# Handing out GpSimd's weight sums one at a time, and moving two small sums in VectorE's queue, in a fused RWKV-5 and SwiGLU kernel

## The chip, the cores and the metric

One core of a Trainium2 chip. The time is device microseconds (us) of one execution. The engines are called TensorE (PE in the profile; PEld is its weight load), VectorE (DVE), ScalarE (ACT) and GpSimd (POOL). A stop is idle time of TensorE in front of an instruction. The granted clock is the share of its full speed that TensorE was given in a stretch; 0.50 is called half clock here. PSUM is the memory that TensorE writes its results to, which VectorE and ScalarE then empty. Work is on the path when the end of the run comes later by as much as the work does.

## The reference

Attention of the RWKV-5 kind over 4 batches of 768 positions with 8 heads of 48, then a gated feed-forward block (384 to 1536 to 384) on the 3072 tokens that come out. All data are float32.

```python
def _attn_ref(r, k, v, w, u):
    B, H, S, D = r.shape                      # 4, 8, 768, 48
    state = np.zeros((B, H, D, D), dtype=np.float32)
    for t in range(S):
        kt, vt, rt = (k[:, :, t], v[:, :, t], r[:, :, t])
        cur = np.einsum('bhd,bhe->bhde', u[None] * kt, vt)
        y[:, :, t] = np.einsum('bhd,bhde->bhe', rt, state + cur)
        state = w[None, :, :, None] * state + np.einsum('bhd,bhe->bhde', kt, vt)

def _moe_ref(x, w_gate, w_val, w_out):
    g = x @ w_gate
    silu = g * (1.0 / (1.0 + np.exp(-g)))
    return (silu * (x @ w_val) @ w_out).astype(np.float32)
```

## The kernel before

Attention is computed in 24 chunks of 128 positions. For each chunk a matrix At of 128x128 per head holds the scores; its diagonal is `du`, the sum over a head's 48 columns of r·k·u. GpSimd forms the product `rk`, VectorE sums it to `du`, and ScalarE writes `ident` times `du` into At. The scores then overwrite one side of At, and the matmuls into `y_ps` use it.

```python
    def own_product(i):
        kl, rl = k_ld[i % 2], r_ld[i % 2]
        rk = two.tile([P, H, D], FP32, name="rk", tag="rk")       # two buffers
        pool.tensor_mul(rk[:], rl[:], kl[:])
        pool.tensor_mul(rk[:], rk[:], ub[:])
        du = three.tile([P, H], FP32, name="du", tag="du")
        dve.tensor_reduce(du[:], rk[:], axis=AX.X, op=ALU.add)
        dus[i] = du

    def diagonal(i):
        du = dus.pop(i)
        ...                                                        # i < 2: on GpSimd
            for h in range(H):
                act.activation(At[i % 2][:, h, :], ident[:], AF.Identity, scale=du[:, h : h + 1])
```

Beside this the weights are rounded in chunks by three engines. ScalarE writes `w_mag` (one buffer) and `w_low`, VectorE a `tensor_scalar` and a `scalar_tensor_tensor` per half, GpSimd the closing addition:

```python
        dve.tensor_scalar(dst, hi, -(1 << 31), None, ALU.bitwise_and)
        dve.scalar_tensor_tensor(
            dst, mags[n][half], 3, dst, ALU.logical_shift_left, ALU.bitwise_or)
        ...
            pool.tensor_tensor(dst, dst, low, ALU.add)
```

Gate units (`gate_value`: six matmuls with `wg`, six with `wv` into `gv`, a sigmoid `sg` on ScalarE, two products `sg` and `hT` on VectorE) fill TensorE's time between. The last projection is done with seven products of halves instead of eight; it needs four sums of weight halves and four of `hT` per pair of chunks, all on GpSimd:

```python
    def weight_sums():
        pool.tensor_sub(wt[1][:], w22, w12)
        pool.tensor_sub(w12, w12, w11)
        pool.tensor_sub(wt[0][:], w22, w12)
        pool.tensor_sub(wt[2][:], w21, wt[0][:])
```

The loop over steps, cut; "F" in `gaps` feeds a unit, "R" rounds a chunk of weights:

```python
    EARLY = {s: ("R", "F", "R", "F", "RF") for s in range(3, 12)}
    ...
    for s in range(3, N + 2):
        if s <= N:
            diagonal(s - 1)
        if s + 1 < N:
            own_product(s + 1)
            scale(s + 1)
        if s < N:
            turn(s)                    # transposes tp, then kT and rT on ScalarE
        gaps(s, 0)
        if s <= N:
            scores(s - 1, 0)
            ...
        gaps(s, 2)
        if s >= 4:
            outputs(s - 2)             # y_ps
            ...
        gaps(s, 4)
        if s == 12:
            count_outside()            # three on VectorE, n_ps on TensorE
        if done["pool"] == NW and not summed:
            weight_sums()
```

## Time and profile before

| what | before |
|---|---|
| time, median of 3 runs | 707.17 us (706.67 to 707.88) |
| span of the profiled execution | 706.3 us |
| TensorE busy, 0 to 195 us | 175.39 of 195.00 us |
| TensorE busy, 195 to 690 us | 495.00 of 495.00 us |
| TensorE busy, 690 us to the end | 10.56 of 16.30 us |

The three stretches are from the table of windows. All slack of TensorE lies in the first and the last; the middle can only get worse. The list of waits and the timelines of the first stretch are shown in the prediction.

### The profile page before, as it was taken

To read this page: it belongs to the slowest core of one execution; us is meant where nothing else is said; L and a number is where in the kernel's file an instruction comes from. 1 tells how busy PE (TensorE), PEld (TensorE's weight loads), DVE (VectorE), ACT (ScalarE), POOL (GpSimd) and SP (SyncE) were. 2 spreads that over 40 slices of the span, in tenths; PEclk is the share of its full clock that TensorE was granted. 3 is DMA by queue.
4 is the path that set the end of the run, shared out by engine and by line. 5 is a ranking of instruction groups with operands and counts; after the bars stand their busy time and mean duration, and the time that the engine had idled before them with its cause. 6 is when DMAs were issued, how large, how long until landed. Compare 5 with 4: busy or idle time off the path is not lost.

```text
span 706.3 us, 11610 instructions
## 1 busy us (share of the span) xinstructions
PE 681.0 (96%) x4822; PEld 620.2 (88%) x4822; DVE 240.7 (34%) x519; ACT 204.4 (29%) x522; POOL 237.1 (34%) x191
## 2 busy tenths in 40 slices
PE   8888997999899999999999999999999999999996
PEld 8777886898798998999999999999898998998996
DVE  5777772313222222323222322323222322222222
ACT  3577762442132231313131331313131211111110
POOL 6877678358203320602512420602400400304000
PEclk9998998999999999999999999999999999999999
DMA  8798831113001010102011110001000000000000
GB/s 236 196 240 226 204 76 34 35 35 78 17 18 46 12 34 23 34 1 57 12 23 35 23 35 23 12 1 35 1 1 23 1 1 23 1 17 7 1 23 26
DMA packets 85774, 34.07 MB, mean 48 GB/s; under 512 B 76368, under 2 KB 79568, under 8 KB 85712
## 3 DMA queue, kind: packets, MB, share of 16 engines
q1 hardware_dynamic: 82256, 28.52, 17.3%
q10 hardware_dynamic: 3456, 4.72, 1.8%
q8 instruction: 40, 0.66, 0.4%
q14 instruction: 22, 0.18, 0.1%
HBM read 28.51 MB, written 4.72 MB: 47 GB/s over the span
## 4 chain that ended last, share of the span: by engine, by line
PE 81%; DVE 6%; POOL 5%; ACT 5%; issue 1%; DMA 1%; SPq 0%; DVEq 0%; POOLq 0%
PE gv L390 47%; PE o_a L453 13%; PE o_b L453 10%; PE y_ps L344 4%; PE s_ps L314 4%; PE tp L300 2%; ACT At L291 2%; ACT w_mag L162 1%; PE u_ps L357 1%; DVE At L318 1%; ACT kT L303 1%; DVE hT L398 1%; DVE sg L397 1%; DVE wg L180 1%; DMA r_ld<-in_r_dram 1%
## 5 line engine op out<-in xcount | busy, mean ns | idle before, releaser
L390 PE MATMUL gv<-xT,wg 128*128 128x256 f32 x864 | 216.0, 387 | 4.0 <-DVE hT L398 4.0
L390 PE MATMUL gv<-xT,wv 128*128 128x256 f32 x864 | 211.6, 381 | 0.0
L390 PEld LDWEIGHTS gv<-xT,wv 128*128 128x128 f32 x864 | 165.5, 192 | 22.9
L390 PEld LDWEIGHTS gv<-xT,wg 128*128 128x128 f32 x864 | 159.7, 193 | 25.8 <-issue 7.7
L397 DVE TENSOR_TENSOR sg<-sg,gv 128x256 f32<-128x256 f32 x144 | 60.5, 420 | 348.2 <-ACT sg L396 347.8
L396 ACT ACTIVATE sg<-gv 128x256 f32<-128x256 f32 x144 | 55.0, 382 | 345.9 <-PE gv L390 345.8
L432 POOL TENSOR_TENSOR hs<-hT 128x768 f32<-128x768 f32 x11 | 19.9, 1809 | 195.6 <-DVE hT L398 195.6
L370 POOL TENSOR_TENSOR Z<-Z,wL 96x384 f32<-96x384 f32 x16 | 15.9, 995 | 191.7 <-DVE Z L369 191.7
L398 DVE TENSOR_TENSOR hT<-sg,gv 128x256 f32<-128x256 f32 x144 | 60.6, 421 | 5.1
L291 ACT ACTIVATE At<-ident,du 128x128 f32<-128x128 f32 x176 | 53.6, 389 | 0.0
L314 PE MATMUL s_ps<-rT,kT 96*128 96x128 f32 x384 | 51.3, 278 | 0.4 <-DVE Z L367 0.4
L453 PE MATMUL o_a<-wt,hs 128*128 128x192 f32 x288 | 50.9, 327 | 0.4 <-ACT u L461 0.4
L314 PEld LDWEIGHTS s_ps<-rT,kT 96*128 96x128 f32 x384 | 49.5, 194 | 1.5 <-DVE Z L367 0.7
L453 PE MATMUL o_b<-wo,hs 128*128 128x192 f32 x288 | 50.7, 326 | 0.0
L453 PEld LDWEIGHTS o_a<-wt,hs 128*128 128x128 f32 x288 | 47.5, 190 | 1.5 <-ACT u L461 0.7
L453 PEld LDWEIGHTS o_b<-wo,hs 128*128 128x128 f32 x288 | 47.6, 190 | 0.8
L318 DVE COPY_PREDICATED At<-mask,s_ps 128x512 f32<-128x512 int32 x48 | 35.0, 733 | 24.4 <-PE s_ps L314 24.4
L344 PE MATMUL y_ps<-At,v_ld 128*32 128x128 f32 x768 | 36.1, 279 | 5.8 <-ACT kT L303 4.4
L344 PEld LDWEIGHTS y_ps<-At,v_ld 128*32 128x32 f32 x768 | 29.9, 111 | 6.6 <-ACT kT L303 4.6
L344 PE MATMUL y_ps<-rT,Z 96*32 96x128 f32 x480 | 30.2, 278 | 1.7 <-ACT kT L303 1.7
L303 ACT ACTIVATE kT<-tp,own 96x512 f32<-96x512 f32 x48 | 29.8, 672 | 0.0
L162 ACT ACTIVATE w_mag<-w_bits 128x384 f32<-128x384 f32 x36 | 19.0, 529 | 24.3 <-DVE wg L180 11.0
(82 smaller groups left out, 639.2 us busy)
## 6 DMA issues: line engine op xcount, KB each, us to landing
k_ld<-in_k_dram SPq DMA_DIRECT2D x24, 192.0 KB, 2.9
r_ld<-in_r_dram SPq DMA_DIRECT2D x24, 192.0 KB, 3.3
w_bits<-in_moe_w_gate_dram SPq DMA_DIRECT2D x6, 768.0 KB, 5.1
v_ld<-in_v_dram SPq DMA_DIRECT2D x48, 96.0 KB, 2.8
w_bits<-in_moe_w_val_dram SPq DMA_DIRECT2D x6, 768.0 KB, 4.7
w_bits<-in_moe_w_out_dram SPq DMA_DIRECT2D x6, 768.0 KB, 4.5
out_dram<-o_sb ACTq DMA_DIRECT2D x24, 192.0 KB, 1.9
ub<-in_u_dram SPq DMA_DIRECT2D x1, 192.0 KB, 3.7
```

The costliest lines, as they stand in the source:

```text
L162: act.activation(mags[n][-1].bitcast(FP32), hi.bitcast(FP32), AF.Abs, scale=float(2.0**-112))
L291: act.activation(At[i % 2][:, h, :], ident[:], AF.Identity, scale=du[:, h : h + 1])
L303: act.activation(kT[i % 2][:, :, e, :], tp[0:D2], AF.Identity, scale=own[:, e : e + 1])
L314: pe.matmul(ps[:, n, :], kT[i % 2][:, a, e, :], turned[i][:, a, :], start=True, stop=True, skip_group_check=True,)
L318: dve.copy_predicated(At[i % 2][:, 4 * half : 4 * half + 4], mask[:].bitcast(INT32).unsqueeze(1).to_broadcast([P, HP, P]), ps[:],)
L344: pe.matmul(ps[32 * q : 32 * q + 32, cc, :], *rows[q][n], start=(n == 0), stop=(n == len(rows[q]) - 1), skip_group_check=True,)
L390: pe.matmul(gv[:, o, :].rearrange("p (i t) -> p i t", i=2), wt[:, c, P * f : P * (f + 1)], xT[:, 2 * g % NX : 2 * g % NX + 2, c, :], start ...
L396: act.activation(sg[:], gv[:, 0, :], AF.Sigmoid)
L397: dve.tensor_mul(sg[:], sg[:], gv[:, 0, :])
L398: dve.tensor_mul(hT[g][:, f, :], sg[:], gv[:, 1, :])
L432: by.tensor_add(s1, h22, h21)
L453: pe.matmul(ps[:], lhs[:, f, :], rhs[:, f, :], start=(f == 0 and n in (0, 1, 4)), stop=(f == FH - 1), skip_group_check=True,)
```

## The change

Its intent: GpSimd's four weight sums and four half sums come in a row and hold what stands behind them. They are handed out one at a time (the half sums two at a time). `du` leaves `own_product` and is made where it is used, so that VectorE doesn't wait for a product that GpSimd has yet to make. The count of w outside the range is made at the very front instead of in step 12.

```diff
     def own_product(i):
         ...
         pool.tensor_mul(rk[:], rk[:], ub[:])
-        du = three.tile([P, H], FP32, name="du", tag="du")
-        dve.tensor_reduce(du[:], rk[:], axis=AX.X, op=ALU.add)
-        dus[i] = du
+        rks[i] = rk
 
     def diagonal(i):
-        du = dus.pop(i)
+        du = three.tile([P, H], FP32, name="du", tag="du")
+        dve.tensor_reduce(du[:], rks.pop(i)[:], axis=AX.X, op=ALU.add)
 ...
-    def weight_sums():
-        (four pool.tensor_sub)
+    def weight_sum():
+        n = len(summed)
+        o = (wt[1][:], w12, wt[0][:], wt[2][:])[n]
+        a, b = ((w22, w12), (w12, w11), (w22, w12), (w21, wt[0][:]))[n]
+        pool.tensor_sub(o, a, b)
+        summed.append(n)
 ...
-    def h_sums(g, by):
+    def h_sums(g, n, by):              # n = 0: s1, s2; n = 1: s3, s4
 ...
             if what == "R":
-                round_weights()
+                if done["pool"] < NW:
+                    round_weights()
+                elif len(summed) < 4:
+                    weight_sum()
 ...
-    EARLY = {s: ("R", "F", "R", "F", "RF") for s in range(3, 12)}
+    EARLY = {s: ("R", "F", "R", "F", "RF") for s in range(3, 13)}
+    dve.tensor_tensor(bad[:], held[:], wcol[:], ALU.not_equal)
+    dve.tensor_reduce(badc[:], bad[:], axis=AX.X, op=ALU.add)
+    dve.memset(ones[:], 1.0)
 ...
         if s == 12:
-            count_outside()
-        if done["pool"] == NW and not summed:
-            weight_sums()
+            (n_ps matmul and its copy alone)
```

More of the change, by code (lines that the diff above doesn't have):

```diff
@@ L195, in round_weights @@
         round_act()
-    dus = {}
+    rks = {}
     def own_product(i):
@@ L370, in update @@
             pool.tensor_mul(z[:], z[:], wL[:].rearrange("p a e d -> p a (e d)"))
-    def count_outside():
-        dve.tensor_tensor(bad[:], held[:], wcol[:], ALU.not_equal)
-        dve.tensor_reduce(badc[:], bad[:], axis=AX.X, op=ALU.add)
-        dve.memset(ones[:], 1.0)
-        n_ps = ps_a.tile([P, HP, P], FP32, name="n_ps", tag="a")
-        pe.matmul(n_ps[0:1, 0, 0:1], badc[:], ones[:], start=True, stop=True)
-        act.copy(outside, n_ps[0:1, 0, 0:1])
     hT = {}
@@ L411, in fast @@
     wt = [cst.tile([P, FH, NH], FP32, name=f"wt{n}") for n in (2, 3, 4)]
-    def weight_sums():
-        pool.tensor_sub(wt[1][:], w22, w12)
-        pool.tensor_sub(w12, w12, w11)
-        pool.tensor_sub(wt[0][:], w22, w12)
-        pool.tensor_sub(wt[2][:], w21, wt[0][:])
+    def weight_sum():
[4 more added lines that the diff above has]
+        summed.append(n)
     part_of = {}
@@ L424, in h_quarters @@
         ]
-    def h_sums(g, by):
-        a, b = (
-            three.tile([P, 2, FH, P], FP32, name=n, tag="w_bits") for n in ("hs12", "hs34")
-        )
+    def h_sums(g, n, by):
         h11, h12, h21, h22 = h_quarters(g)
-        s1, s2, s3, s4 = a[:, 0], a[:, 1], b[:, 0], b[:, 1]
-        by.tensor_add(s1, h22, h21)
-        by.tensor_sub(s2, s1, h11)
-        by.tensor_sub(s3, h11, h21)
-        by.tensor_sub(s4, h12, s2)
-        part_of[g] = {"s": (s1, s2, s3, s4)}
+        if n == 0:
+            a, b = (
+                three.tile([P, 2, FH, P], FP32, name=n, tag="w_bits") for n in ("hs12", "hs34")
+            )
+            part_of[g] = {"s": (a[:, 0], a[:, 1], b[:, 0], b[:, 1])}
+        s1, s2, s3, s4 = part_of[g]["s"]
+        if n == 0:
+            by.tensor_add(s1, h22, h21)
+            by.tensor_sub(s2, s1, h11)
+        else:
+            by.tensor_sub(s3, h11, h21)
+            by.tensor_sub(s4, h12, s2)
     def project(g, n):
@@ L486, in queue @@
     def queue(g):
-        parts = [(NW + 1, lambda p=p: project(g - 1, p)) for p in range(7)] if g > 1 else []
+        parts = [(NW + 4, lambda p=p: project(g - 1, p)) for p in range(7)] if g > 1 else []
         if g == 2:
-            todo.append((NW + 1, lambda: h_sums(0, pool)))
-            todo.extend((NW + 1, lambda p=p: project(0, p)) for p in range(7))
+            for p in range(7):
+                if p < 2:
+                    todo.append((NW + 4, lambda p=p: h_sums(0, p, pool)))
+                todo.append((NW + 4, lambda p=p: project(0, p)))
         for f in range(FC):
-            need = 2 * (f // 2) + 2 if g < 2 else NW + 1
+            need = 2 * (f // 2) + 2 if g < 2 else NW + 4
             todo.append((need, lambda f=f: gate_value(g, f)))
-            if parts and f == 0:
-                todo.append((NW + 1, lambda: h_sums(g - 1, pool)))
+            if parts and f < 2:
+                todo.append((NW + 4, lambda f=f: h_sums(g - 1, f, pool)))
             if parts and 2 <= f < 9:
@@ L570, in fast @@
         if s == 12:
-            count_outside()
-        if done["pool"] == NW and not summed:
-            summed.append(True)
-            weight_sums()
+            n_ps = ps_a.tile([P, HP, P], FP32, name="n_ps", tag="a")
+            pe.matmul(n_ps[0:1, 0, 0:1], badc[:], ones[:], start=True, stop=True)
+            act.copy(outside, n_ps[0:1, 0, 0:1])
     assert done["pool"] == NW
     feed(len(todo))
-    h_sums(N // 2 - 1, dve)
+    h_sums(N // 2 - 1, 0, dve)
+    h_sums(N // 2 - 1, 1, dve)
     for p in range(7):
```

## The prediction

> **What bounds the kernel now.** I read the page first, then the list of waits, then the timeline of each engine between 0 and 240 us, because the change touches the front of the run most. The page's busy row says which engine to follow:
>
> ```profile
> PE 681.0 (96%) x4822; PEld 620.2 (88%) x4822; DVE 240.7 (34%) x519; ACT 204.4 (29%) x522; POOL 237.1 (34%) x191
> ```
>
> TensorE is busy 681.0 of 706.3 us. In the table by stretches it is busy 495.00 of 495.00 us between 195 and 690 us, at full clock: nothing can be gained there, only lost. All that a change of waits can win is in the first 195 us. The list of waits gives TensorE's stops, and the waits of VectorE that lie behind them (columns: total us, times, longest us):
>
> ```profile
> DVE du L205 <- POOL rk L203: 32.1, 9, 11.0
> ...
> PE y_ps L344 <- ACT kT L303: 6.1, 3, 4.4
> ...
> PE gv L390 <- DVE hT L398: 4.0, 1, 4.0
> ...
> PE n_ps L378 <- DVE ones L376: 1.8, 1, 1.8
> ...
> PE tp L300 <- DVE At L318: 1.7, 1, 1.7
> ```
>
> The first row is the target of the change: the sum du stands in VectorE's queue right behind the product rk that GpSimd has yet to make, so whatever holds GpSimd holds VectorE. The timelines show the worst case: four weight sums in a row on GpSimd, then the product rk behind them, then du, and TensorE waiting for a PSUM buffer that VectorE should have emptied (columns: start, length, then the instruction; in brackets the idle time before it):
>
> ```profile
> 104.83 2.62 POOL L414 TENSOR_TENSOR wt<-wo 128x1152 f32<-128x1152 f32 x1
> 107.53 2.63 POOL L415 TENSOR_TENSOR wo<-wo 128x1152 f32<-128x1152 f32 x1
> 110.24 2.64 POOL L416 TENSOR_TENSOR wt<-wo 128x1152 f32<-128x1152 f32 x1
> 112.95 2.63 POOL L417 TENSOR_TENSOR wt<-wo,wt 128x1152 f32<-128x1152 f32 x1
> ```
>
> ```profile
> 117.63 0.55 DVE L205 TENSOR_REDUCE du<-rk 128x8 f32<-128x384 f32 x1 [11.00 <-POOL rk L203]
> ```
>
> ```profile
> 119.72 2.90 PE L390 MATMUL gv<-xT,wg 128*128 128x256 f32 x6 [4.00 <-DVE hT L398]
> 122.41 2.77 PE L390 MATMUL gv<-xT,wv 128*128 128x256 f32 x6
> ```
>
> The last two rows also show a second cost: six such matmuls take 1.46 us elsewhere, here 2.90 and 2.77.
>
> The other stage that matters runs from about 37 to 105 us, while the weights are being rounded. There VectorE and ScalarE hand halves of each chunk to each other, and TensorE waits for ScalarE (4.43 us at 55.34, 1.17 us at 83.82, 0.52 us at 97.45: the 6.1 us above). One step of the loop, from the timelines of VectorE and ScalarE:
>
> ```profile
> 80.95 0.42 DVE L398 TENSOR_TENSOR hT<-sg,gv 128x256 f32<-128x256 f32 x1
> 81.29 0.55 DVE L205 TENSOR_REDUCE du<-rk 128x8 f32<-128x384 f32 x1
> ...
> 84.70 0.56 DVE L180 SCALAR_TENSOR_TENSOR wo<-w_mag,wo 128x384 int32<-128x384 int32 x1 [1.87 <-ACT w_mag L162]
> ```
>
> ```profile
> 79.93 0.37 ACT L396 ACTIVATE sg<-gv 128x256 f32<-128x256 f32 x1
> 80.19 2.43 ACT L291 ACTIVATE At<-ident,du 128x128 f32<-128x128 f32 x8
> 82.53 1.24 ACT L303 ACTIVATE kT<-tp,own 96x512 f32<-96x512 f32 x2
> ```
>
> ScalarE starts At at once after sg, since its du was made a step earlier or more; VectorE then waits 1.87 us for ScalarE's w_mag. So ScalarE's chain At, kT, rT, w_mag sets the pace of this stage.
>
> **What the Trainium skill says.** "TensorE: Matmul & The Clock Gate", Part 1 (What's actually happening): the PE clock goes to half rate after an idle window of about 3.4 us and back after a busy one, and the window is free-running. The trace agrees: granted clock 0.50 from 119.7 to 125 us after the stop of 4.00 us, and 0.50 from 55.3 to 60.5 after 4.43; the stops of 1.8 and 1.7 us bring none. The same page, Part 1 (Architectural detail), calls ScalarE's and VectorE's queues strict FIFO, which is why one du can hold all evictions; the 11.00 us agree. "SBUF — State Buffer", Who interferes with whom: `tensor_scalar` on VectorE and GpSimd's instructions exclude each other. The trace has such a case (a TENSOR_SCALAR at 92.97 us that takes 2.29 us instead of 0.35 to 0.43 while GpSimd works from 92.20 to 95.04); I assume the change makes no more and no fewer of them.
>
> **The change part by part.** The order of instructions of both builds says that no work is added or removed: the same matmuls, 24 du, four weight sums, the same half sums.
>
> 1. Weight sums, one at a time. After the change the first stands where all four stood; the next product rk, which stood behind 4 x 2.63 us, comes 2.6 us later instead, and nothing of VectorE's waits for it in that step. The stop of 4.00 us goes, and the half clock after it: from 119.72 to the next transposes at 124.97 us is 5.25 us for one gate unit that takes 2.59 at full clock, 2.66 lost. 4.0 + 2.7 = 6.7, of which 0.3 comes back because the PSUM slot for y_ps waits for kT. Gain 6.4 us.
>
> 2. du at the place of its use. In every step du now stands in VectorE's queue where the du two steps ahead stood, so its rk is ready; but ScalarE's At in the same step now waits for it. At could start after sg; now it starts after VectorE's sg, hT and du. Delay = (start of hT + 0.42 + 0.55) - (start of At before), step by step from the timelines: 40.46 - 39.24 = 1.2 (here du alone), 53.89 - 51.71 = 2.2, 67.90 - 66.17 = 1.7, 81.92 - 80.19 = 1.7, 97.25 - 93.81 = 3.4. Sum 10.2 us on the chain that paces the stage. Against it, at the very front VectorE no longer waits 2.71 us for rk at 26.77, and both steps there have no du; followed through w_mag and the next du this is about 1.8 us at the first At. Net 8.4 us if the loop is rigid. It isn't wholly: VectorE's idle 1.3 to 1.9 us per step gives GpSimd's instructions a place without collisions, and TensorE's spare time takes a part. I choose 7. The stops of TensorE that grow in it (about 6, 1.4, 3 and 4 us) cause half clock once more, perhaps: 1 us. Loss 8 us.
>
> 3. The same move of du with less load. At 160.30 a du waits 10.35 us behind the eight additions for the seven products; this is the stop of 1.7 us of tp. It goes, but y_ps then waits 0.7 us for kT: gain 1.0. Later, ScalarE is free enough: At starts some 1.4 us later (hT and du), with 1.3 to 1.5 us of slack before y_ps at 130.57 and 143.6 us: loss 0.2. In one later step three gate units follow the transposes directly; the third needs a PSUM buffer freed by a sigmoid behind At: loss 1.0.
>
> 4. The count moved to the front: 0.32 + 0.15 + 0.06 us on VectorE's queue, where two du of 0.5 us each go away. No difference. At its old place TensorE no longer stops 1.82 us: gain 1.85.
>
> 5. Step 12 has three feeds instead of twelve, and units move to the tail. TensorE's work is the same and the tail is dense: 0.
>
> Sum: -6.4 + 8.0 - 1.0 + 0.2 + 1.0 - 1.85 = -0.05 us. On the 707.17 us measured: 707.1, I say 707.
>
> **The rivals.** (a) *At is not on the path, or its delay is absorbed.* Then the 8 us are not lost and the front gains: 707.2 - 6.4 - 1.0 - 1.85 - 1 = about 697. For it: VectorE has 32.1 us of waits on rk, all removed. Against it: only 11.00, 10.35 and 2.71 us of these are seen near a stop, and VectorE waits for w_mag, not ScalarE for VectorE's du. Chance about 0.3.
> (b) *The delays are rigid, and the half clock strikes twice.* 10.2 - 1.8 + 2 x 2.7 = 13.8 instead of 8: about 713. For it: stops of 3 to 4 us are near the length that brought half clock at 119.7. Against: while the clock is half, TensorE's idle time shrinks, so the same time isn't lost twice. Chance about 0.2.
> (c) *GpSimd's new write-after-read wait*: rk has two buffers, and the product for a later chunk now waits until VectorE has summed the one two before. It moves GpSimd by up to 2 us in a step where its products are wanted a step later; if it delayed the additions that finish the weights, the gate matmuls would stop. I see GpSimd waiting 2 us per chunk for VectorE there, so it has room: under 1 us.
>
> **How range and chances follow.** The middle is rivals (a) and (b) around a sum near zero: 707. From (a) at 697 and (b) at 713, with three in ten and two in ten, 8 times in 10 the time lies between 697.5 and 713. Two per cent is 14.1 us. To be faster by that much would need all of the recoverable waits of the front (1.8 + 1.7 + 6.7 + 4.4 + its half clock 2.7) and no new one: 0.03. Slower by that much would need (b) and more: 0.03. Within 2%: 0.94.
>
> **What would show each step right or wrong.** In the profile after: no wait of du on rk over 1 us, and the gate unit near 119 us at full clock without a stop (1); ScalarE's At waiting for VectorE's du, some 1.5 to 3.5 us in each step before 110 us, and y_ps's wait for kT grown from 6.1 to some 12 to 15 us (2); no stop at n_ps (4); the transposes that began at 105.14 now beginning near 112, those that began at 124.97 near 126. If At has no wait for du, or those transposes begin before 106, step 2 is wrong and rival (a) holds. If TensorE shows stops after 195 us of over 2 us, my reading of the later steps is wrong.

## The result, and the profile after

The changed kernel takes 711.36 us (median of 4 runs, 710.25 to 711.73) against 707.52 us (706.67 to 708.63) for the kernel before in the same rounds. The ratio is 1.0051, with a 95% interval from 1.0032 to 1.0070: within 2%, and a little slower. A ratio is the mean time of one kernel's fast runs over the mean of the other's fast runs in the same rounds, so it isn't quite the ratio of the medians quoted. Where runs of different rounds are compared below, I use (ratio − 1) × 707 us, "over before" for short: +3.6 us here. One such figure is known to 1.0 to 1.3 us, a difference of two to about 1.7 us (an estimate from the intervals), so differences under that are read from the traces.

TensorE's work is the same, but the page's busy row of the changed kernel shows 1.5 us more for the same count of matmuls (681.0 before), and the mean granted clock of the profiled execution is 0.983 instead of 0.988: more of it ran at half clock.

```profile
PE 682.5 (96%) x4822; PEld 621.0 (87%) x4822; DVE 240.9 (34%) x519; ACT 205.4 (29%) x522; POOL 237.0 (33%) x191
```

The list of waits of the changed kernel (columns: total us, times, longest us):

```profile
POOL rk L202 <- DVE du L282: 48.7, 15, 5.0
...
ACT At L290 <- DVE du L282: 31.2, 19, 3.3
...
PE y_ps L343 <- ACT kT L302: 12.9, 4, 4.9
...
PE gv L380 <- DVE hT L388: 1.2, 1, 1.2
```

VectorE's 32.1 us of waiting for `rk` are gone, as intended. In their place ScalarE waits 31.2 us for `du`, and GpSimd 48.7 us, because it may not write `rk` again before VectorE has summed the product that lies in that buffer. TensorE's stop at `gv` of 4.0 us is gone, and those at `n_ps` (1.8) and `tp` (1.7); its stops at `y_ps` grew from 6.1 to 12.9 us. So of these stops 6.3 us were taken away (7.5, less a new stop of 1.2), and 6.8 put back.

How that comes about is seen in one step, on the timelines of ScalarE and VectorE of the changed kernel (start, length, instruction, in brackets the idle time before it and what ended it). It is the step that the prediction shows for the kernel before, from 80 us on:

```profile
84.22 0.36 ACT L386 ACTIVATE sg<-gv 128x256 f32<-128x256 f32 x1
86.14 2.45 ACT L290 ACTIVATE At<-ident,du 128x128 f32<-128x128 f32 x8 [1.56 <-DVE du L282]
88.49 1.24 ACT L302 ACTIVATE kT<-tp,own 96x512 f32<-96x512 f32 x2
```

```profile
85.56 0.54 DVE L282 TENSOR_REDUCE du<-rk 128x8 f32<-128x384 f32 x1
...
90.68 0.56 DVE L180 SCALAR_TENSOR_TENSOR wo<-w_mag,wo 128x384 int32<-128x384 int32 x1 [4.30 <-ACT w_mag L162]
```

`du` stands at the same place in VectorE's queue as before, but it is now the `du` that At of this very step needs. At starts 1.56 us after ScalarE is free; kT, rT and w_mag follow it in ScalarE's queue, and VectorE, which has nothing else to do, waits 4.30 us for w_mag instead of 1.87. If ScalarE's chain sets the pace, each step is longer by what At waits; the experiments test that.

The starts of the transposes of two steps, on TensorE's timeline, first the kernel before (steps 8 and 9):

```profile
105.14 0.60 PE L300 MATMUL tp<-ident,khat 128*96 128x128 f32 x4
...
124.97 0.85 PE L300 MATMUL tp<-ident,khat 128*96 128x128 f32 x4
```

and the changed kernel, from the stop in step 7 on, with one row of a much later step:

```profile
107.16 0.66 PE L343 MATMUL y_ps<-rT,Z 96*32 96x128 f32 x8 [4.26 <-ACT kT L302]
...
110.30 2.78 PE L380 MATMUL gv<-xT,wg 128*128 128x256 f32 x6
...
117.52 0.60 PE L299 MATMUL tp<-ident,khat 128*96 128x128 f32 x4
...
130.55 0.60 PE L299 MATMUL tp<-ident,khat 128*96 128x128 f32 x4
...
396.91 1.53 PE L380 MATMUL gv<-xT,wg 128*128 128x256 f32 x6 [1.16 <-DVE hT L388]
```

Up to step 8 the change loses 12.38 us (117.52 − 105.14). From step 8 to step 9 it gains 6.80 us: 13.03 us instead of 19.83, since the stop behind the four sums is gone. The gate unit at 110.30 shows a new half clock, 2.78 us for six matmuls that take 1.46 at full clock.

### The profile page after: what moved, and what is told of

Its sections match the earlier page's. It is cut to its first block, busy times and chain, and to the rows that moved or that the text cites. A ratio compares the mean times of both kernels' runs of the same rounds, so it can differ in the third digit from the quotient of the medians.

```text
span 709.8 us, 11598 instructions
## 1 busy us (share of the span) xinstructions
PE 682.5 (96%) x4822; PEld 621.0 (87%) x4822; DVE 240.9 (34%) x519; ACT 205.4 (29%) x522; POOL 237.0 (33%) x191
## 4 chain that ended last, share of the span: by engine, by line
PE 82%; DVE 9%; ACT 5%; POOL 1%; issue 1%; DMA 0%; DVEq 0%; SPq 0%; POOLq 0%
PE gv L380 48%; PE o_a L448 13%; PE o_b L448 10%; PE y_ps L343 5%; PE s_ps L313 4%; ACT At L290 2%; PE tp L299 2%; PE u_ps L356 1%; DVE At L317 1%; ACT kT L302 1%; DVE hT L388 1%; DVE wv L179 1%; DVE sg L387 1%; DVE wv L180 1%; DVE wg L180 1%
## 5 line engine op out<-in xcount | busy, mean ns | idle before, releaser
L290 ACT ACTIVATE At<-ident,du 128x128 f32<-128x128 f32 x176 | 53.8, 388 | 31.6 <-DVE du L282 31.2
L202 POOL TENSOR_TENSOR rk<-r_ld,k_ld 128x384 f32<-128x384 f32 x24 | 24.1, 1006 | 53.0 <-DVE du L282 48.7
```

## The experiments

Theory 1, formed from the two traces: the wait of At for `du` in the same step sets the pace of steps 3 to 7 and costs what it lasts; handing out the sums is a gain by itself. Rivals: the loss comes from handing out the sums, or from GpSimd waiting to write `rk` again, or from half clock alone. Twelve kernels were run, each in five rounds beside the kernel before on the same chip. All gave the right result.

### The parts by themselves

**e1_du_back**: the changed kernel, with `du` back at its old place.

```diff
     def own_product(i):
         ...
+        du = three.tile([P, H], FP32, name="du", tag="du")
+        dve.tensor_reduce(du[:], rk[:], axis=AX.X, op=ALU.add)
+        dus[i] = du
     def diagonal(i):
-        du = three.tile(...); dve.tensor_reduce(du[:], rks.pop(i)[:], ...)
+        du = dus.pop(i)
```

> The changed kernel with the sum du back at its old place (right behind the product rk of the chunk two steps ahead), the one-at-a-time weight sums and the moved count kept. Theory 1 (the loss is At waiting for du while the weights are rounded): the transposes of step 8 begin near 105 us again instead of 117.5, no wait of At for du, the stop at 119 us stays away or is under 1 us, the time is near 699 us (696 to 702), clearly below both kernels. Rival (the loss comes from handing the sums out, or from the units moved into the tail): the time stays near 711.

Measured: 698.39 us against 707.1, ratio 0.9871 (0.9856 to 0.9886), 9.1 us under before. ScalarE has no wait for `du` in front of any At. The row of the At of step 7, and the transposes of step 8:

```profile
94.17 2.44 ACT L291 ACTIVATE At<-ident,du 128x128 f32<-128x128 f32 x8
```

```profile
105.49 0.60 PE L300 MATMUL tp<-ident,khat 128*96 128x128 f32 x4
```

Step 8 begins at 105.49 us, as in the kernel before (105.14). So the 12.38 us belong to the move of `du`, and the other parts gain. In this run `du` still waits 28.2 us in all for `rk` (32.1 before), and yet it is 9.1 us faster: most of the wait that the move was to take away cost little.

**e2_du_only**: the kernel before with the move of `du` alone.

```diff
     def own_product(i):
-        du = three.tile(...); dve.tensor_reduce(du[:], rk[:], ...); dus[i] = du
+        rks[i] = rk
     def diagonal(i):
-        du = dus.pop(i)
+        du = three.tile(...); dve.tensor_reduce(du[:], rks.pop(i)[:], ...)
```

> The kernel before with the move of du alone; the four weight sums in a row and the count at its old place stay. Theory 1 says that the move of du takes away the stop of 4 us by itself, since no du waits behind the four sums any more, and brings the loss of the rounding stage: transposes of step 8 near 117.5 us, no wait of du on rk, the stop at n_ps still there, time near 713 us (711 to 715). Rival (the stop of 4 us goes because the sums are handed out one at a time): the stop and its half clock remain behind the four sums, time near 719 us.

Measured: 717.29 us against 707.1, ratio 1.0138 (1.0122 to 1.0153), +9.8 us. The time missed the range that theory 1 gave. From the list of waits of this kernel:

```profile
ACT At L290 <- DVE du L282: 31.2, 20, 3.3
...
PE y_ps L343 <- ACT kT L302: 13.6, 4, 4.9
```

and from TensorE's timeline, the transposes of step 12:

```profile
168.17 0.64 PE L299 MATMUL tp<-ident,khat 128*96 128x128 f32 x4 [1.34 <-POOL khat L272]
```

The mechanism is as theory 1 says: the stop of 4.00 us at `gv` doesn't occur, even with the four sums still in a row, because `du` no longer waits for the product behind them; transposes of step 8 at 118.06, of step 9 at 131.54. But sums that still come in a row now stop TensorE elsewhere: 1.34 us at 168.17, behind four half sums, and 0.32 at the transposes after it. The stop of 1.6 at `n_ps` is that of the count at its old place (1.8 before); 2.1 us at `o_a` (0.4 before) were not followed to their cause. The lesson of this run is that handing out the sums and moving `du` each remove the same stop. Together they remove it once.

**e3_sums_only**: the kernel before, with the sums handed out and nothing else (the hunks of `weight_sum`, `h_sums`, `queue`, `gaps`, `EARLY`).

```diff
-        if done["pool"] == NW and not summed:
-            weight_sums()
+                elif len(summed) < 4:          # in gaps, where "R" stands
+                    weight_sum()
```

> The kernel before with the sums for the seven products handed out one at a time, du and the count as before. Theory 1: du behind rk waits some 3 to 4 us instead of 11 in the step of the first weight sum, the stop of TensorE of 4 us and its half clock go, time near 700.5 us (698 to 703). Rival (handing out gains nothing by itself): near 707.

Measured: 699.45 us against 707.1, ratio 0.9886 (0.9871 to 0.9901), 8.1 us under before. The stop at `gv` is gone; the longest wait of `du` for `rk` is 6.8 us, longer than I expected, but it no longer stops TensorE.

**e4_count_only**: the kernel before with the count at the front, `n_ps` and its copy left in step 12.

```diff
+    dve.tensor_tensor(bad[:], held[:], wcol[:], ALU.not_equal)
+    dve.tensor_reduce(badc[:], bad[:], axis=AX.X, op=ALU.add)
+    dve.memset(ones[:], 1.0)
     warm(14)
```

> The kernel before with the count alone moved to the front. Both theories: the stop of 1.82 us before n_ps goes, time near 705.3 us (704.5 to 706.5), 0.3 per cent faster. If the count at the front delays the first rounding on VectorE and that counts, it is 707 or more.

Measured: 705.35 us against 707.1, ratio 0.9979 (0.9965 to 0.9992), 1.5 us under before.

The sum of these: −8.1 − 1.5 is −9.6, and with both parts at once (e1) −9.1. The move of `du` adds 9.8 to the kernel before, and 12.7 to e1 (3.6 + 9.1): there it has no stop left to remove.

### What the move of du costs, and by what

**e7_du_twice**: the changed kernel, with the sum of five chunks (2 to 6) made twice. If At's wait is on the path, each doubling costs its length.

```diff
+        for _ in range(2 if 2 <= i <= 6 else 1):
             dve.tensor_reduce(du[:], rk[:], axis=AX.X, op=ALU.add)
```

> The changed kernel with du of the chunks 2 to 6 computed twice in a row (same result): 0.46 us more on VectorE in each of the five steps of the rounding stage. Theory 1 (ScalarE's At waits for du and paces the stage, rigidly): 5 x 0.46 = 2.3 us longer, 713 to 714.5 us. Rival (VectorE's spare 4 us per step there take it up): 711.4, at most 0.5 us more.

Measured: 714.40 us against 707.36, ratio 1.0097 (1.0081 to 1.0112), +6.9 us, that is 3.3 more than the changed kernel (3.0 by the medians). The pair takes 1.13 us on VectorE instead of 0.54, so five times 0.59 = 2.95 was to be added. The transposes of step 8 begin at 120.54, 3.02 us later than in the changed kernel: nothing of it is absorbed.

**e6_rk3**: the changed kernel with three buffers for `rk`, so that GpSimd needs no leave from VectorE.

```diff
-        rk = two.tile([P, H, D], FP32, name="rk", tag="rk")
+        rk = three.tile([P, H, D], FP32, name="rk", tag="rk")
```

> The changed kernel with three buffers for rk instead of two. Theory 1: GpSimd's waits for du (48.7 us in total) go, and the time stays at 711.4 (710 to 712.5), since GpSimd has room. Rival (GpSimd's new wait is the cost of the move): 700 to 705 us.

Measured: 708.89 us against 707.36, ratio 1.0025 (1.0011 to 1.0039), +1.8 us, 1.8 less than the changed kernel (2.5 by the medians), which is hardly more than the uncertainty; in the traces the transposes of step 8 come 2.58 us earlier (114.94). That was a miss: I expected no change, so theory 1 is not the whole cause. GpSimd's timeline in the changed kernel shows the wait, in the step shown above:

```profile
86.19 1.04 POOL L202 TENSOR_TENSOR rk<-r_ld,k_ld 128x384 f32<-128x384 f32 x1 [3.35 <-DVE du L282]
```

It makes GpSimd late, and its weight addition then lies where VectorE wants to run a `tensor_scalar`. Rows of step 7 of the changed kernel, GpSimd and VectorE:

```profile
107.53 1.83 POOL L190 TENSOR_TENSOR wo<-wo,w_low 128x768 int32<-128x768 int32 x1
```

```profile
108.50 1.08 DVE L179 TENSOR_SCALAR wo<-w_bits 128x384 int32<-128x384 int32 x1
```

The same two of the kernel with three buffers:

```profile
104.02 1.83 POOL L190 TENSOR_TENSOR wo<-wo,w_low 128x768 int32<-128x768 int32 x1
```

```profile
106.99 0.35 DVE L179 TENSOR_SCALAR wo<-w_bits 128x384 int32<-128x384 int32 x1
```

In the changed kernel the addition ends at 109.36 and the `tensor_scalar`, begun at 108.50, at 109.58: it stood still until GpSimd was done. With three buffers the addition is over at 105.85, and the same instruction takes 0.35 us. The Trainium skill, "SBUF — State Buffer", Who interferes with whom, says of VectorE's modes with two ports, which `tensor_scalar` can enter, that the first to issue holds the shared ports for the whole instruction and the other "fully blocks"; this pair agrees, with 1.08 us against 0.35. In the changed kernel this instruction behind w_mag takes 1.08 to 1.11 us in each of the steps 3 to 7, with three buffers 0.35 to 0.42, and it stands on the chain, since ScalarE's next w_mag waits for VectorE to empty the one buffer. The kernel before has such a block in each of these steps too, but at the `tensor_scalar` right behind `du` (0.68 to 1.08 us; 0.35 to 0.41 there in the changed one). In the step that the prediction shows:

```profile
81.75 1.08 DVE L179 TENSOR_SCALAR wo<-w_bits 128x384 int32<-128x384 int32 x1
```

There VectorE waits 1.87 us for w_mag afterwards (1.28 to 2.61 in steps 3 to 6), so the block is hidden. From 34 to 110 us, 11 of these instructions take more than 0.6 us in the kernel before, and 10 in the changed one: the blocks didn't become more, they moved from in front of a wait to behind it.

**e8_fill**: the changed kernel, with 16 matmuls of no use (`ident` on `ident`) at step 7's stop, to keep the clock up.

```diff
+        if s == 7:
+            fill = ps_o.tile([P, P], FP32, name="fill", tag="o")
+            for _ in range(16):
+                pe.matmul(fill[:], ident[:], ident[:], start=True, stop=True)
         if s >= 4:
             outputs(s - 2)
```

> The changed kernel with 16 dummy matmuls on TensorE in the stop of 4.26 us before y_ps of step 7, into a PSUM buffer that nobody uses there. Theory 1's term of the half clock: without the idle window the clock stays at full rate behind the stop, the y_ps and the gate unit from 107.2 to 112.9 us take 3.1 instead of 5.7 us, time 2 to 3 us shorter (708.5 to 709.5). If the half clock there is not on the path or does not come from the stop: no difference or, if the dummies outlast the stop, longer.

Measured: 710.03 us against 707.36, ratio 1.0037 (1.0023 to 1.0051), +2.6 us: only 1.0 less than the changed kernel, half of what I expected. The granted clock between 107 and 113 us rose from 0.52 to 1.00, but in this run step 6 was struck instead (0.57 between 90 and 94 us, after a stop of 3.34 us). By itself it settles little. The matmuls of no use, which the trace records as 32, also outlast the stop:

```profile
104.93 3.74 PE L571 MATMUL fill<-ident 128*128 128x128 f32 x32
...
108.59 0.43 PE L343 MATMUL y_ps<-rT,Z 96*32 96x128 f32 x8
```

Here y_ps begins 4.27 us after At, in the changed kernel 3.65 (107.16 − 103.51).

**e10_fill3**: the same at three stops: 7, 7 and 16 such matmuls in steps 5, 6 and 7.

```diff
+        if s in {5: 7, 6: 7, 7: 16}:
+            fill = ps_o.tile([P, P], FP32, name="fill", tag="o")
+            for _ in range({5: 7, 6: 7, 7: 16}[s]):
+                pe.matmul(fill[:], ident[:], ident[:], start=True, stop=True)
```

> The changed kernel with dummy matmuls in the stops before y_ps of the steps 5, 6 and 7 (7, 7 and 16 of them). In e8 the fill at step 7 alone took the half clock away there, while the half clock struck at step 6 instead. With all three filled I expect no half clock from 70 to 115 us, the transposes of step 8 some 2 to 3 us earlier than in the changed kernel (114.5 to 115.5), time 708.5 to 709.5 us. If the half clock costs nothing on the path: 711.

Measured: 709.19 us against 707.15, ratio 1.0024 (1.0010 to 1.0037), +1.7 us, 1.9 less than the changed kernel (2.2 by the medians). Two stretches from the table of windows (window, length, then busy time and count of PE, PEld, DVE, ACT and POOL, then granted clock, DMA share, GB/s), first of the changed kernel, then of this one:

```profile
75.00:79.00 4.00, 4.00 (x12) 3.17 (x12) 3.86 (x8) 2.48 (x5) 2.72 (x2) 0.57 0.75 184
...
107.00:113.00 6.00, 5.84 (x63) 4.79 (x64) 4.13 (x7) 3.04 (x7) 4.19 (x3) 0.52 0.35 70
```

```profile
75.00:79.00 4.00, 3.89 (x22) 3.39 (x23) 3.86 (x8) 2.64 (x5) 2.87 (x2) 1.00 0.74 163
...
107.00:113.00 6.00, 5.65 (x79) 5.06 (x80) 4.59 (x9) 3.54 (x8) 4.43 (x3) 1.00 0.34 67
```

Both half-clock stretches of the changed kernel (0.57 and 0.52) are at full clock. Step 6 (86 to 94 us) is at 1.00 in both.

**e12_rk3_fill3**: both cures, three buffers for `rk` and matmuls of no use in steps 5, 6 and 7 (sized to the stops that e6 showed).

```diff
-        rk = two.tile([P, H, D], FP32, name="rk", tag="rk")
+        rk = three.tile([P, H, D], FP32, name="rk", tag="rk")
 ...
+        if s in {5: 5, 6: 12, 7: 9}:
+            (as in e10)
```

> The changed kernel with both cures at once: three buffers for rk, and dummy matmuls of about 1.2, 2.8 and 2.1 us in TensorE's stops before y_ps of steps 5, 6 and 7 (sized from the stops of 1.39, 3.19 and 2.29 us that the run with three buffers showed). By themselves the cures brought 2.5 us (three buffers) and 2.2 us (dummy matmuls). If collisions and half clock are separate costs, the sum stands: about 706.7 us, 706.2 to 707.2. If they are partly one and the same cost (the run with three buffers already had a granted clock of 0.81 instead of 0.52 between 107 and 113 us), it is only 708 to 709. What is then left over the version with du at its old place (698.4) is what At waits for du, 9.5 us in steps 3 to 7 less 1.5 of the front: 8.

Measured: 707.15 us against 708.14 (means 0.9994, interval 0.9980 to 1.0007), −0.4 us over before, 4.0 less than the changed kernel; the two cures alone gave 1.8 and 1.9. So they add up, as nearly as runs of different chips can tell. The At of step 7 and the transposes of step 8 in this run:

```profile
102.78 2.45 ACT L290 ACTIVATE At<-ident,du 128x128 f32<-128x128 f32 x8 [3.28 <-DVE du L282]
```

```profile
114.11 0.60 PE L299 MATMUL tp<-ident,khat 128*96 128x128 f32 x4
```

The timelines give a finer account, in which the front of a run can be set apart; each row is one profiled execution. Start of At in steps 3 and 7, start of the transposes of step 8, all in us; "waits" is the sum of At's waits in steps 4 to 7:

| kernel | At 3 | At 7 | transposes 8 | At 3 to At 7 | waits in it | At 7 to transposes |
|---|---|---|---|---|---|---|
| e1, du back | 39.58 | 94.17 | 105.49 | 54.59 | 0 | 11.32 |
| changed | 38.85 | 103.51 | 117.52 | 64.66 | 8.44 | 14.01 |
| e6, three rk | 39.02 | 102.01 | 114.94 | 62.99 | 8.45 | 12.93 |
| e10, fills | 38.93 | 103.71 | 115.04 | 64.78 | 8.46 | 11.33 |
| e12, both | 39.78 | 102.78 | 114.11 | 63.00 | 8.44 | 11.33 |

From At 3 to At 7, e12 takes 8.41 us more than e1, and At waits 8.44 us in it: At's wait is paid in full. The changed kernel takes 10.07 more, so 1.63 us beyond the waits; with three buffers this excess is gone, so it is GpSimd's. From At 7 on, the changed kernel takes 2.69 us longer than e1; with fills this is gone, so it is half clock. With three buffers it is 1.61, since the clock fell for a shorter time there (0.81 between 107 and 113 us). The front gives 0.73 back (38.85 against 39.58), although At waits 1.08 us in step 3 already. This term is the least certain: At 3 begins at 38.85, 38.93 and 39.51 in the changed kernel, e10 and e8, which don't differ up to there. 8.44 + 1.63 + 2.69 − 0.73 = 12.03 us, which is 117.52 − 105.49. That account also explains the poor result of e8: its At 3 began at 39.51, 0.66 us later than in the changed kernel, before the edit could act, and its way from At 7 to the transposes took 11.96 us, so 2.05 of the 2.69 were gained there; the missing 0.6 is what the matmuls of no use outlasted the stop by. The fill of step 5 gained nothing: from At 3 to At 7 e10 takes 64.78 us, the changed kernel 64.66.

### A better place for du

**e5_between**: the changed kernel, with `du` at the same place in VectorE's queue but for the chunk in between: its `rk` was made one step earlier, and its At comes one step later.

```diff
+    def own_sum(i):
+        du = three.tile([P, H], FP32, name="du", tag="du")
+        dve.tensor_reduce(du[:], rks.pop(i)[:], axis=AX.X, op=ALU.add)
+        dus[i] = du
     def diagonal(i):
-        du = three.tile(...); dve.tensor_reduce(du[:], rks.pop(i)[:], ...)
+        du = dus.pop(i)
     ...
         if s <= N:
             diagonal(s - 1)
+        if s < N:
+            own_sum(s)
         if s + 1 < N:
             own_product(s + 1)
```

(and `own_sum` for chunks 0, 1 and 2 ahead of the loop).

> The changed kernel with du at the same place in VectorE's queue, but for the chunk in between: its product rk was made one step earlier, its At comes one step later. Theory 1 (both old and new place make somebody wait, VectorE for rk or ScalarE for du, and only that costs): no wait of du on rk over 1 us and no wait of At on du over 0.5 us, transposes of step 8 at or before 105 us, time at or a little below that of the changed kernel with du back (698.4): 695 to 698.5 us. Rival (the rounding stage is slower for another reason that comes with a du that is not the newest, such as collisions of GpSimd and VectorE): well above 700.

Measured: 697.33 us against 707.36, ratio 0.9858 (0.9843 to 0.9874), 10.0 us under before: the best placing tried, ahead of both kernels. ScalarE's and VectorE's timelines in the step shown above:

```profile
78.28 0.36 ACT L390 ACTIVATE sg<-gv 128x256 f32<-128x256 f32 x1
78.55 2.43 ACT L294 ACTIVATE At<-ident,du 128x128 f32<-128x128 f32 x8
```

```profile
79.63 0.55 DVE L208 TENSOR_REDUCE du<-rk 128x8 f32<-128x384 f32 x1
...
83.06 0.56 DVE L180 SCALAR_TENSOR_TENSOR wo<-w_mag,wo 128x384 int32<-128x384 int32 x1 [1.88 <-ACT w_mag L162]
```

`du` has no idle time before it, At none, and VectorE's wait for w_mag is 1.88 us again. The list of waits has no row of `du` on `rk`, of ScalarE's At on `du` or of `rk` on `du`; GpSimd waits once, 0.6 us, for the `du` of an At that it makes ahead of the loop. From At 3 to At 7 it takes 54.56 us, as long as e1 (54.59). What it is ahead of e1 by, 0.9 us, comes from the front, where At 3 begins at 37.61 instead of 39.58.

**e9_between_twice**: e5 with the sums of chunks 2 to 6 made twice, as in e7.

```diff
     def own_sum(i):
+        for _ in range(2 if 2 <= i <= 6 else 1):
             dve.tensor_reduce(du[:], rk[:], axis=AX.X, op=ALU.add)
```

> The kernel of e5 (du for the chunk in between) with du of the chunks 2 to 6 computed twice, as e7 did to the changed kernel, where it cost 3.0 us. Theory 1: here nobody waits for that du in its step and VectorE waits for w_mag behind it anyway, so it costs at most 0.5 us: 697.3 to 697.9 us. Rival (the doubling costs VectorE time that paces the stage in any case): 3 us, 700.3.

Measured: 697.04 us against 707.15, ratio 0.9855 (0.9840 to 0.9870). The same 2.95 us that cost 3.3 in e7 cost nothing here: with a step of room on either side, `du` is off the path.

**e11_between_fill4**: e5 with 16 matmuls of no use at its longest stop before `y_ps`, in step 4.

```diff
+        if s in {4: 16}:
+            (as in e10)
```

> The kernel of e5 with 16 dummy matmuls in the stop of 4.46 us before y_ps of step 4. Theory 1: the half clock behind that stop is not on the path, since TensorE waits for ScalarE again at the next y_ps: no difference, 697.3 within 0.5 us. If TensorE's half clock counts there: about 2 us less.

Measured: 697.21 us against 707.15, ratio 0.9859 (0.9843 to 0.9874), no difference from e5, although the granted clock between 53 and 60 us rose to 1.00, from 0.76 in e5 and 0.55 in e9. So half clock cost nothing here and in step 5 of the changed kernel, and 2.7 us in its step 7, where TensorE had no slack behind it.

## Why the prediction was right or wrong

The time, 711.36 us, lies in the range and within 2%. The centre was 4.4 us too low, and of its five parts one failed: part 2. The numbers below are those of the prediction's parts; a "step" is one of the loop.

1. *Weight sums one at a time, gain 6.4.* Right. If the gain of 1.0 at 160 us, which part 3 put down to `du`, is counted here, 7.4 was predicted for handing out the sums; e3 gained 8.1. The stop at `gv` went, as foretold.
2. *du at the place of its use, loss 8.* Main mechanism right, size wrong: 12.0 us up to step 8, and of the 4 us missing, 1.6 are a cost that was seen and dismissed. Its terms:
   - At's waits, predicted as 1.2, 2.2, 1.7, 1.7 and 3.4 (10.2), were 1.08, 2.04, 1.57, 1.56 and 3.27 (9.52). Less the front's gain, foretold as 1.8 and measured as 1.81 (0.73 + 1.08, to about 0.7), this makes 7.7. I had 8.4, from waits read a little too long (I added whole durations, and in the trace hT begins at 80.95, takes 0.42 and is followed at 81.29), and then took off 1.4 because the loop would give way. It gave way nowhere (e7, e12), so this discount had no ground; that the first error made up for half of it was luck.
   - Half clock, "perhaps: 1 us", was 2.69. I argued that TensorE's idle time would shrink while the clock is half. In step 7 the transposes of step 8 follow the gate units without a stop, so the whole stretch is on the path.
   - GpSimd's new wait for leave to write `rk`, rival (c), "under 1 us", was 1.63, and 1.08 of the half clock went with it in e6. I looked for a delay of the weights' end and found room. I didn't ask where GpSimd's later instruction would then lie. The prediction even quotes the exclusion of `tensor_scalar` and GpSimd, and assumes that the change makes "no more and no fewer" such cases. Their number did stay nearly the same (11 and 10). What failed is the thought that only the number counts: one per step came from in front of VectorE's wait for w_mag, where it was hidden, onto the chain behind it.
3. *The later steps.* The stop of `tp` went (gain 1.0). Steps 9 and 10 lost nothing (0.2 predicted: 13.03 us from step 9 to step 10, 13.29 before). The one later stop, predicted as 1.0, is that of 1.16 us at 396.91.
4. *The count, gain 1.85.* Right: e4 gained 1.5 (1.75 by the medians).
5. *The tail, 0.* Right: after 690 us TensorE is idle for 5.98 us (19.80 − 13.82), before for 5.74.

Without part 2's move the prediction makes 6.4 + 1.0 + 1.85 = 9.25 us of gain, and e1 measured 9.1. With it, 8 + 1.2 predicted against 12.7 measured, and the account above has 12.0 + 1.16, within the 1.7 us to which such differences are known. Rival (b), rigid delays with half clock twice (713), was nearest in size, in part by luck: it has 5.4 us of half clock where 2.7 were measured, and no block by GpSimd. Rival (a) is refuted by e1 and e7. Of the signs named, no wait of `du` on `rk`, At's waits (1.08 to 3.27 us), y_ps's wait of 12 to 15 us (12.9), no stop at `n_ps` and no stop over 2 us after 195 us came true; "near 112" and "near 126" for the transposes did not (117.52 and 130.55), while the step between them took 13.03 us against the 14 foretold. The gain of part 1 is real; it went into part 2's move.

What stays open: why half clock followed a stop of 1.85 us in step 5 of the changed kernel and not one of 2.10 us in step 5 of e8 (where the stop in step 6 then lasted 3.34 us instead of 1.94, and was struck); and the size of each cure to better than about 1.7 us in run time, since the changed kernel ran in other rounds than its variants and the finer account has one execution of each.

## What to carry to other kernels

In a software pipeline of in-order queues, put a small link between two engines a whole step behind its producer and a whole step ahead of its consumer: the same sum at the same place in the same queue cost 12.7 us as its consumer's last-minute input, and nothing one chunk later. When a change removes a wait, ask which engine now does the waiting, and also what the engine that is made late will lie beside when it does run: a wait with "room" still shifted GpSimd's addition onto VectorE's `tensor_scalar`. And when two parts of a change remove the same stop, count its gain once and test each part alone; here the second fix had no stop left to take away in step 8, and cost more (12.7 us) than the first had gained (8.1). A long total in the list of waits is no reason to act by itself: of VectorE's 32.1 us of waits for `rk`, e1 kept 28.2 and was 9.1 us faster than the kernel before; e5, without them, gained only 0.9 more.

## What the Trainium skill lacked or had wrong

- "TensorE: Matmul & The Clock Gate", Part 1 (What's actually happening), gives an idle window of about 3.4 us before half rate. In the changed kernel a stop of 4.26 us was followed by half clock (0.52 from 107 to 113 us), but so was one of 1.85 us at 73.72 (0.57 from 75 to 79 us), while one of 1.94 us at 89.79 was not. The page calls the window free-running, which leaves the moment uncertain; for the short stops that it does mention, those that come often, it gives no length, so a reader can't tell that one of half the window's length can be struck. The prediction, with two such stops in the trace of before that were not, took them as harmless.
- The same page doesn't say that half clock may be free: e11 lifted it in step 4 (0.76 and 0.55 to 1.00) for no gain, e10 lifted it in step 5 for none (64.78 us from At 3 to At 7 instead of 64.66) and in step 7 for 2.7 us.
- "SBUF — State Buffer", Who interferes with whom, is right about the block (1.08 us instead of 0.35 for a `tensor_scalar`). It does not have a consequence that cost 1.63 us in four steps here: an engine made late by a wait can move such a block from a place where it is hidden onto the chain, with no wait to be seen in the list, since the blocked instruction only looks longer.
